# Attention's instructions and early transfers in the order of a table, 68 of them on another engine, three filler matmuls fewer

## The chip, the cores and the metric

The kernel runs on one core of a Trainium2 chip. The core has engines that each work through a queue of their own, in order: TensorE (PE, with the loading of weights shown as PEld), VectorE (DVE), ScalarE (ACT), GpSimd (POOL), and SyncE (SP), which issues nearly all transfers. The metric is the time of one execution on the device in microseconds (us), as the median of several runs.

## The reference

Attention over a window of 16 to either side and over one summary for each block of 32 positions (the maximum of the keys, the mean of the values), and behind it two expert layers with the same shape and different activations.

```python
def _attn_ref(q, k, v):                       # q, k, v: 2 x 8 x 768 x 64
...
    k_sum = k.reshape(B, H, nb, block, D).max(axis=3)
    v_sum = v.reshape(B, H, nb, block, D).mean(axis=3)
    scores_l = scale * np.matmul(q, k.transpose(0, 1, 3, 2))
...
    mask_l = np.abs(pos[:, None] - pos[None, :]) < window
    scores_s = scale * np.einsum('bhsd,bhnd->bhsn', q, k_sum)
    scores_s = scores_s + np.log(block)
...
    a = np.exp(scores_all)
    a = a / (np.sum(a, axis=-1, keepdims=True) + 1e-09)
...
    return np.matmul(a, v_all).astype(np.float32)

def _moe_ref(x, w_in, w_out):                 # x: 1536 x 512, d_ff 2048
    h = x @ w_in
    r = np.maximum(h, 0.0)
    g = r * r
    return (g @ w_out).astype(np.float32)

def _moe2_ref(x, w_in, w_out):
    h = x @ w_in
    g = h * (1.0 / (1.0 + np.exp(-1.702 * h)))
    return (g @ w_out).astype(np.float32)
```

## The kernel before

The kernel doesn't issue an instruction when its code is written. Each piece of work is an operation in a plan (`Plan.op`): an engine, a duration that the plan assumes, a function that issues the instructions, and the buffers it reads and writes. The plan gives every operation a start time by its own rules, and `emit` sorts all of them by that start and calls their functions. So the start times decide one thing alone: the order of the instructions in each engine's queue. What an instruction waits for follows from its buffers. Where several engines could do a piece of work, `soonest` takes the choice that the plan expects to end first. Operations are numbered (`seq`) in the order in which they are planned. Numbers 0 to 1199 are attention, the steps of the first expert layer that stand between its pieces, and the beginning of what follows.

The string `ORDER` lists the pieces of the front. Those that the text speaks of:

- `K`, `B`, `q`, `k`, `V`, `v`: transfers of parts of k, q and v. `T`, `tq`, `tk`: transposes on PE (L646 for k's first six blocks, L604 for q and k) and the copies from PSUM to `kw` and `qT`. `tq,1` is the second block of q, in two halves.
- `g,i,h`: for block i of 128 queries and half h of the heads the scores on PE (L735), the maximum passes on DVE (L750, each one operation a head, with its read-out), the exponentials of four heads on ACT (L765), the reciprocal (L779) and the multiply (L772) of the softmax. `h,i,h` is the same with all scores at once.
- `t,i`: transposes of the weights (L802), copies to `pT`, the weighted sum on PE (L814), and its split into a rounded part `xh` and a rest `xl` (L827).
- `w,f,z`: block f of an expert's weights: a transfer to `raw`, ACT scales it (L923), DVE joins parts (L927, L932), and ACT or DVE split it into a rounded `w` and a rest (L958 or L959, L963).
- `s,f,h` and `S,f`: one step of the first expert layer over half h of 512 tokens, or over all: 12 matmuls to `h` (L998), relu and square (L1012 to L1019), the rounded activations `gh` (L1026, L1027) and their low half `gl` (L1029), and one step later 12 matmuls to `acc` (L1053).

From 168 us on, the rest of both expert layers runs.

PE also gets filler matmuls, which multiply the identity by itself into a bank that nobody reads yet, so that PE is at work where the plan has gaps: `fill` puts them into gaps of the plan, and `WARM` adds groups at two given times. One filler is two matmuls in the trace (tile `warm`, L1774). The fillers need the identity, which POOL makes.

The lines behind the copies of the front, as an example of a choice of engines:

```python
    def copy(out, src, ps, key, cost=0.48):
        plan.soonest([("ACT", cost, False, lambda: nc.scalar.copy(out=out(), in_=src())),
                      ("DVE", cost * 1.26, False, lambda: nc.vector.tensor_copy(out=out(), in_=src()))],
                     reads=[(ps, 0)], writes=[*key, (ps, 0)])
```

Of the kernel before, what the change touches and what calls it, by code (L numbers as in the profile page):

```python
# [38 lines left out]
}  # L39
LAST = (2,), (0, 1), (3,)  # L40
SHAKE = (14, 0.15)
WARM = (15.52, 6), (21.24, 5)
KEPT = 10
LOW3 = 7.4999 / 2.0 ** 32
LESS = 99.0
# [91 lines left out]


class Op:
    __slots__ = ("eng", "start", "end", "fn", "seq", "far")  # L140


class Plan:
# [93 lines left out]
    def soonest(self, choices, reads=(), writes=(), after=()):  # L237


        best = None  # L240
        deps = self._deps(reads, writes, after)
        for eng, dur, port, fn in choices:
            if eng == "POOL" and port and self.alone:
                continue
            lines = (eng, "PORT") if port else (eng,)
            dur *= self.slack[1] if eng == "POOL" else 1.0
            end = self._place(lines, self._ready(eng, deps), dur) + dur
            if eng == "DVE":
                end += self.lean[0] if choices[0][0] == "ACT" else self.lean[1]
            if best is None or end < best[0]:  # L250
                best = end, eng, dur, port, fn
        _, eng, dur, port, fn = best
        return self.op(eng, dur, fn, reads=reads, writes=writes, after=after, port=port)

    @staticmethod
    def _deps(reads, writes, after):
# [43 lines left out]
                self.ops.append(o)  # L300

    def emit(self):
        for o in sorted(self.ops, key=lambda o: (o.start, o.seq)):
            o.fn()

# [2 lines left out]
def kernel(  # L308
# [1466 lines left out]

    plan.fill(0.27, keep_warm, first_ops["acc3"], WARM)
    with tc.manual_schedule():
# [30 lines left out]
```

## Time and profile before

| | us |
|---|---|
| median of 3 runs | 567.78 (567.07 to 567.97) |
| the profiled execution | 568.08 |
| its span, first to last instruction | 566.4 |
| PE busy in the span | 560.2 |
| DVE busy | 495.6 |
| ACT busy | 412.7 |
| POOL busy | 41.8 |

The span is the time between the first and the last instruction of the profiled execution; 1.7 us of that execution lie around it. Busy times are those of the whole span; the front of the kernel, up to some 35 us, looks different from the rest, and is read by stretches further down. A busy PE includes its fillers, and the ends of matmuls are modelled.

### The profile page before, as it was taken

The numbers are of one execution on the slowest core, as the hardware profiler recorded it, in microseconds if no ns is written. First come the engines' busy times: TensorE is split into PE (matmuls) and PEld (weight loads), VectorE is DVE, ScalarE is ACT, GpSimd is POOL, SyncE is SP. The second block draws the span as 40 slices with busy tenths as digits, with TensorE's granted clock in tenths as the row PEclk, the third lists the DMA queues.
The fourth block names the chain that finished last, engine by engine and source line by source line (L and its number), as shares of the span: only waits on it lengthen the run. The fifth ranks groups of instructions, "written<-read, shape, count | busy, mean of one in ns | idle before, by whom it ended". The sixth has DMA issues, their size and how long they took to land.

```text
span 566.4 us, 11027 instructions
## 1 busy us (share of the span) xinstructions
PE 560.2 (99%) x3838; PEld 481.3 (85%) x3838; DVE 495.6 (88%) x1110; ACT 412.7 (73%) x899; POOL 41.8 (7%) x112
## 2 busy tenths in 40 slices
PE   8999999999999999999999999999999999999997
PEld 8889988888878887888888888888888888899997
DVE  4788898888889899989999899998999999789974
ACT  4899889898896668777789757477366676677650
POOL 6143311211100000000000000000000000000000
PEclk9999999999999999999999999999999999999999
DMA  9999999886677864545558657576255555686723
GB/s 273 247 270 281 273 267 302 262 216 198 208 238 259 269 221 148 182 152 168 186 181 282 206 168 235 185 241 199 92 203 187 176 200 191 213 286 205 222 90 112
DMA packets 104663, 120.26 MB, mean 212 GB/s; under 512 B 28736, under 2 KB 72512, under 8 KB 104608
## 3 DMA queue, kind: packets, MB, share of 16 engines
q1 hardware_dynamic: 104416, 119.17, 67.1%
q0 software_dynamic: 192, 0.39, 0.4%
q8 instruction: 30, 0.49, 0.4%
q14 instruction: 25, 0.20, 0.1%
HBM read 86.64 MB, written 32.51 MB: 210 GB/s over the span
## 4 chain that ended last, share of the span: by engine, by line
PE 94%; SPq 1%; DMA 1%; DVE 1%; ACT 1%; issue 0%; DVEq 0%; ACTq 0%
PE acc L1440 14%; PE m L1440 12%; PE h L998 10%; PE acc L1053 8%; PE acc L1347 8%; PE acc L1345 7%; PE m L1345 5%; PE acc L998 5%; PE m L1347 4%; PE m L1055 4%; PE acc L1055 3%; PE h L1347 2%; PE h L1345 2%; PE m L802 2%; PE m L814 2%; PE m L998 1%
## 5 line engine op out<-in xcount | busy, mean ns | idle before, releaser
L963 DVE TENSOR_TENSOR w<-xw,w 128x512 fp32r<-128x512 f32 (+1 forms) x141 | 83.9, 609 | 2.7 <-ACT w L958 2.0
L958 ACT CAST w<-xw 128x512 fp32r<-128x512 f32 (+1 forms) x127 | 68.5, 552 | 23.0 <-DVE xw L932 15.9
L998 PE MATMUL h<-xh,w 128*128 128x512 f32 (+1 forms) x184 | 55.6, 364 | 0.0
L1440 PE MATMUL m<-top,w 128*128 128x512 f32 x210 | 53.5, 391 | 0.1
L932 DVE SCALAR_TENSOR_TENSOR xw<-raw,xw 128x512 uint32<-128x512 uint32 x67 | 45.8, 689 | 4.6 <-ACT raw L923 2.7
L923 ACT ACTIVATE raw<-raw 128x512 f32<-128x512 f32 x72 | 47.7, 679 | 1.0 <-DMA raw<-in_moe_w_in_dram 0.8
L1440 PEld LDWEIGHTS m<-top,w 128*128 128x128 f32 x210 | 38.7, 188 | 8.2 <-ACT r L363 0.5
L1440 PE MATMUL acc<-top,w 128*128 128x512 f32 x174 | 43.9, 390 | 0.0
L1053 PE MATMUL acc<-gh,w 128*128 128x512 f32 (+1 forms) x160 | 42.6, 353 | 0.0
L1440 PE MATMUL acc<-xh,w 128*128 128x512 f32 x124 | 42.1, 389 | 0.0
L1440 PEld LDWEIGHTS acc<-top,w 128*128 128x128 f32 x174 | 32.4, 188 | 6.5
L998 PEld LDWEIGHTS h<-xh,w 128*128 128x128 f32 x184 | 33.1, 189 | 5.6 <-issue 1.0
L765 ACT ACTIVATE sm<-sm,st 128x120 f32<-128x120 f32 x96 | 36.6, 385 | 0.2
L927 DVE TENSOR_SCALAR xw<-raw 128x512 uint32<-128x512 uint32 x67 | 29.1, 438 | 6.8 <-DMA raw<-in_moe_w_in_dram 5.4
L998 PE MATMUL h<-xl,w 128*128 128x512 f32 (+1 forms) x92 | 32.5, 353 | 0.0
L958 ACT CAST top<-gs 128x512 fp32r<-128x512 f32 x38 | 23.5, 618 | 11.3 <-DVE gs L947 3.0
L1053 PEld LDWEIGHTS acc<-gh,w 128*128 128x128 f32 x160 | 27.7, 189 | 4.4 <-issue 0.3
L963 DVE TENSOR_TENSOR top<-gs,top 128x512 fp32r<-128x512 f32 x41 | 27.9, 685 | 2.8 <-ACT top L958 2.6
L1347 PE MATMUL acc<-w,gh 128*128 128x256 f32 x136 | 28.0, 283 | 0.0
L1053 PE MATMUL acc<-gl,w 128*128 128x512 f32 (+1 forms) x80 | 27.8, 348 | 0.0
L1440 PEld LDWEIGHTS acc<-xh,w 128*128 128x128 f32 x124 | 23.3, 188 | 4.8
L998 PE MATMUL acc<-xh,w 128*128 128x512 f32 x80 | 26.1, 389 | 0.0
(300 smaller groups left out, 1501.6 us busy)
## 6 DMA issues: line engine op xcount, KB each, us to landing
raw<-in_moe_w_in_dram SPq DMA_DIRECT2D x36, 512.0 KB, 4.7
raw<-in_moe_w_out_dram SPq DMA_DIRECT2D x36, 512.0 KB, 4.6
w<-xw SPq DMA_DIRECT2D x50, 256.0 KB, 2.3
xw<-w SPq DMA_DIRECT2D x27, 256.0 KB, 2.8
w<-w SPq DMA_DIRECT2D x24, 256.0 KB, 2.8
r<-g SPq DMA_DIRECT2D x17, 256.0 KB, 3.7
vw<-in_v_dram SPq DMA_DIRECT2D x20, 192.0 KB, 4.7
g<-w SPq DMA_DIRECT2D x14, 256.0 KB, 2.0
```

Of the source, the lines that this page charges most:

```text
L765: nc.scalar.activation(out=s.t[:, h, :], in_=s.t[:, h, :], func=AF.Exp, bias=st.t[:, 0, h:h + 1], scale=-1.0, accum_out=st.t[:, 1, h:h + 1])
L923: nc.scalar.activation(out=top, in_=top, func=AF.Prelu, scale=-(2.0 ** -80), alpha=-(2.0 ** -32))
L927: plan.soonest([("DVE", 0.36, True, lambda: nc.vector.tensor_scalar(out=x.t, in0=raw.t[:, :, 0], scalar1=29, scalar2=None, op0=ALU.logical ...
L932: op("DVE", 0.64, lambda: nc.vector.scalar_tensor_tensor(out=x.t, in0=raw.t[:, :, 1], scalar=3, in1=x.t, op0=ALU.logical_shift_left, op1=A ...
L958: plan.soonest([("ACT", 0.09 + 0.44 * fr, False, lambda: nc.scalar.copy(out=hi.t[:, hc], in_=src())), ("DVE", 0.05 + 0.4 * fr, True, lambd ...
L963: eng.tensor_tensor(out=lo.t[:, lc], in0=src(), in1=hi.t[:, hc].bitcast(F32), op=ALU.subtract)
L998: nc.tensor.matmul(hp.t[:, cols], lhsT=w.t[:, kc * P:(kc + 1) * P], rhs=x.t[:, kc, cols], start=(kc == 0 and n == 0), stop=(kc == KC - 1 a ...
L1053: nc.tensor.matmul(a.t[:, cols], lhsT=w.t[:, j * P:(j + 1) * P], rhs=g.t[:, cols], **st)
L1055: nc.tensor.matmul(a.t, lhsT=g.t[:, j * P:(j + 1) * P], rhs=w.t, **st)
L1345: nc.tensor.matmul(b.t, lhsT=w.t[:, x + j * P:x + j * P + P], rhs=g.t, **st)
L1347: nc.tensor.matmul(b.t[:, (j % 2) * CH:(j % 2) * CH + CH], lhsT=g.t[:, j * P:j * P + P], rhs=w.t[:, x:x + CH], **st)
L1440: nc.tensor.matmul(bank.t, lhsT=a, rhs=rhs(b, kh), start=(begin and k == 0 and n == 0), stop=(k == 1 and n == 2), skip_group_check=True)
```

## The change

Two tables are added. `SHIFT` gives 1160 of the operations 0 to 1199 an offset that is added to the planned start before the sort, so it moves them in the queues of all engines, transfers included. `PICK` names 68 operations that were given to `soonest`, and takes the choice with that number instead: 35 go from ACT to DVE, 8 from DVE to ACT, 15 from DVE to POOL, 9 from POOL to DVE, one from POOL to ACT. The second group of `WARM` has two fillers instead of five. Buffers and banks of PSUM are still given out in planning, before the offsets, so who shares a buffer with whom stays as it was.

```diff
-WARM = (15.52, 6), (21.24, 5)
+WARM = (15.52, 6), (21.24, 2)
+SHIFT = {0: 1.001, 1: 1.499, 2: 4.8, 3: -0.749, 4: -4.578, 5: -1.226, 6: -0.7, 7: 0.111, 9: 0.101, 10: 6.4, 11: -0.9,
...
+PICK = {8: 1, 15: 1, 17: 1, 86: 1, 95: 0, 100: 0, 102: 0, 146: 0, 171: 1, 176: 1, 198: 1, 199: 1, 220: 0, 265: 1, 285:
...
 class Op:
-    __slots__ = ("eng", "start", "end", "fn", "seq", "far")
+    __slots__ = ("eng", "start", "end", "fn", "seq", "far", "alts")
...
-        return self.op(eng, dur, fn, reads=reads, writes=writes, after=after, port=port)
+        o = self.op(eng, dur, fn, reads=reads, writes=writes, after=after, port=port)
+        o.alts = choices
+        return o
...
     def emit(self):
+        for o in self.ops:
+            o.start += SHIFT.get(o.seq, 0.0)
+            if o.seq in PICK:
+                o.eng, _, _, o.fn = o.alts[PICK[o.seq]]
         for o in sorted(self.ops, key=lambda o: (o.start, o.seq)):
             o.fn()
```

Three places in the queues follow, as they stand in a row before and after. The line numbers of after are higher by 129 to 133, since the tables take lines.

The first is PE's queue around the transposes of q's second block (`m` from `qin`, L604 before, L733 after), with the scores of block 1 ahead of them. Before:

```order
L735 MATMUL acc_292<-kw,qT_283 64x120
L735 MATMUL m_294<-kw,qT_283 64x120
L1774 MATMUL warm<-ident 128x128 x6
L604 MATMUL m_318<-ident,qin_255 64x128 x8
L604 MATMUL m_329<-ident,qin_255 64x128 x8
L735 MATMUL acc_347<-kw,qT_283 64x120
L735 MATMUL h_349<-kw,qT_283 64x120
```

And after:

```order
L864 MATMUL acc_309<-kw,qT_284 64x120
L864 MATMUL m_311<-kw,qT_284 64x120
L733 MATMUL m_319<-ident,qin_211 64x128 x8
L1903 MATMUL warm<-ident 128x128 x6
L733 MATMUL m_336<-ident,qin_211 64x128 x8
L864 MATMUL acc_355<-kw,qT_284 64x120
L864 MATMUL acc_357<-kw,qT_284 64x120
```

The six fillers of the first group of `WARM` stood ahead of both halves and stand between them now. The scores of `g,0,1` (to `acc_347` and `h_349` before) have gone ahead of the transposes.

The second is DVE's queue at the same time, where the maximum passes of `g,1,0` (`sm_343`, in after `sm_351`) and of `g,0,1` (`sm_390`, in after `sm_376`) begin. Before:

```order
L963 TENSOR_TENSOR w_373<-xw_308,w_357 128x512
L750 ISA sm_343,st_344<-m_294,mask_74 128x120
L750 ISA st_344 128x1
L750 ISA sm_343,st_344<-m_294,mask_74 128x120
L750 ISA st_344 128x1
L750 ISA sm_390,st_391<-acc_347,mask_75 128x120
L750 ISA st_391 128x1
L750 ISA sm_390,st_391<-acc_347,mask_75 128x120
```

And after:

```order
L879 ISA sm_351,st_352<-m_311,mask_74 128x120
L879 ISA st_352 128x1
L493 COPY qT_372<-m_336 128x256
L879 ISA sm_376,st_377<-h_297,mask_75 128x120
L879 ISA st_377 128x1
L879 ISA sm_376,st_377<-h_297,mask_75 128x120
L879 ISA st_377 128x1
L879 ISA sm_351,st_352<-acc_355,mask_74 128x120
...
L879 ISA sm_376,st_377<-acc_295,mask_75 128x120
```

The copy of the second half of q's second block (`m_336`) was ACT's and stands on DVE now, ahead of the two passes of `g,0,1` and of the first of `g,1,1` (`acc_355`), which has gone between those two. The two subtractions of weights (L963) follow later.

The third is DVE's queue where the half-width steps `s,2,0` and `s,2,1` get their activations. In the row of before, the squares (`r`) and casts (`gh`) of these steps are ACT's (L1017, L1027), the subtractions (`gl`) POOL's (L1029), and DVE has weights and the softmax of block 5. After:

```order
L1061 SCALAR_TENSOR_TENSOR xw_1073<-raw_888,xw_1073 128x512
L1148 TENSOR_TENSOR r_1075<-r_1075 128x256
L1155 CAST gh_1090<-r_1075 128x256
L1158 TENSOR_TENSOR gl_1095<-r_1075,gh_1090 128x256
L1092 TENSOR_TENSOR w_1099<-xw_1073,w_1097 128x512
L1056 TENSOR_SCALAR xw_1114<-raw_972 128x512
L1148 TENSOR_TENSOR r_1119<-r_1119 128x256
L1061 SCALAR_TENSOR_TENSOR xw_1114<-raw_972,xw_1114 128x512
L1155 CAST gh_1140<-r_1119 128x256
L1158 TENSOR_TENSOR gl_1152<-r_1119,gh_1140 128x256
```

Six of the eleven half-width instructions that DVE gets in these steps are seen here, among the preparation of weights that was there before.

## Rows read from the trace of the kernel before

**Rows 1.** The page: the chain that ended last, shares of the span by engine.

```profile
PE 94%; SPq 1%; DMA 1%; DVE 1%; ACT 1%; issue 0%; DVEq 0%; ACTq 0%
```

**Rows 2.** Stretches: length, then PE, PEld, DVE, ACT, POOL busy; PEclk, DMA.

```profile
17.20:34.50 17.30, 17.18 (x330) 15.02 (x330) 14.27 (x83) 16.10 (x67) 4.89 (x12) 1.00 1.01 232
34.50:76.70 42.20, 42.19 (x461) 38.86 (x456) 35.65 (x93) 37.21 (x102) 15.23 (x28) 1.00 1.00 279
```

**Rows 3.** Timeline of PE, 0 to 24 us: start, length, line, tiles, count.

```profile
1.43 2.93 PE L1774 MATMUL warm<-ident 128*128 128x128 f32 x12 [1.43 <-POOL band L391]
4.29 1.12 PE L646 MATMUL acc<-ident,kin 128*64 128x128 f32 x8
...
8.12 1.97 PE L646 MATMUL acc<-ident,kin 128*64 128x128 f32 x32 [0.27 <-DMA kin<-in_k_dram]
...
14.96 1.60 PE L1774 MATMUL warm<-ident 128*128 128x128 f32 x12
17.21 1.97 PE L604 MATMUL m<-ident,qin 128*64 128x128 f32 x32 [0.65 <-DMA qin<-in_q_dram]
...
22.18 1.38 PE L1774 MATMUL warm<-ident 128*128 128x128 f32 x10
```

**Rows 4.** Timeline of ACT, 17 to 29 us.

```profile
21.27 0.39 ACT L765 ACTIVATE sm<-sm,st 128x120 f32<-128x120 f32 x1
...
28.30 0.59 ACT L363 COPY pT<-h 120x512 f32<-120x512 f32 x1
```

**Rows 5.** Timeline of DVE, 5 to 21 us.

```profile
5.36 0.48 DVE L927 TENSOR_SCALAR xw<-raw 128x512 uint32<-128x512 uint32 x1 [5.36 <-DMA raw<-in_moe_w_in_dram]
...
19.91 0.28 DVE L750 CUSTOM_DVE_ANT_0 sm<-acc,mask 128x120 f32<-128x120 f32 x1 [0.82 <-PE h L735]
...
20.12 0.28 DVE L750 CUSTOM_DVE_ANT_0 sm<-acc,mask 128x120 f32<-128x120 f32 x1
```

**Rows 6.** Groups by form, 0 to 170 us: count, busy us, mean ns.

```profile
L963 DVE TENSOR_TENSOR w<-xw,w 128x512 fp32r<-128x512 f32 x34 | 23.9, 711 | 2.5 <-ACT w L958 2.0
L772 DVE TENSOR_TENSOR sm<-sm,st 128x480 f32<-128x480 f32 x18 | 12.4, 691 | 1.8
L959 DVE CAST w<-xw 128x512 fp32r<-128x512 f32 x10 | 4.3, 426 | 1.4 <-PE h L998 1.1
L364 DVE COPY kw<-m 64x512 f32<-64x512 f32 x1 | 0.7, 683 | 0.0
L1014 DVE TENSOR_SCALAR r<-h 128x256 f32<-128x256 f32 x1 | 0.4, 418 | 0.0
...
L1029 POOL TENSOR_TENSOR gl<-r,gh 128x256 fp32r<-128x256 f32 x8 | 6.4, 799 | 14.1 <-ACT gh L1027 6.2 <-issue 3.9 <-PE acc L1053 3.0
```

**Rows 7.** Timelines of DVE and PE around 77 us.

```profile
75.97 0.68 DVE L1029 TENSOR_TENSOR gl<-r,gh 128x512 fp32r<-128x512 f32 x1
...
77.60 0.39 PE L1053 MATMUL acc<-gl,w 128*128 128x512 f32 x1
```

**Rows 8.** DVE's waits for ACT and POOL, 34.5 to 76.7 us: total us, times, longest.

```profile
DVE xw L932 <- ACT raw L923: 1.0, 2, 0.5
DVE w L963 <- ACT w L958: 0.8, 2, 0.5
DVE ks L683 <- ACT kw L363: 0.4, 1, 0.4
DVE st L779 <- POOL st L769: 0.4, 2, 0.2
```

**Rows 9.** The chain, 80 to 100 us: start, length, what, count.

```profile
90.13 2.94 PE h L998 x12
93.08 2.72 PE acc L1053 x12
```

**Rows 10.** Timelines of DVE and POOL around 38 us.

```profile
38.02 1.33 DVE L963 TENSOR_TENSOR w<-xw,w 128x512 fp32r<-128x512 f32 x1 [0.29 <-ACT w L958]
...
37.81 0.99 POOL L772 TENSOR_TENSOR sm<-sm,st 128x480 f32<-128x480 f32 x1 [0.30 <-DVE st L779]
```

121 rows, old and new, of tables (PICK, SHIFT) are left out of this document.

## The prediction

> **What bounds the kernel now.** I read the page's chain first [rows 1]: 94% of what ended last is TensorE (PE). Then the table by stage [rows 2]: from 34.5 us on the sum of PE's work is the whole stretch (42.19 of 42.20 us before 76.7 us), and the granted clock reads 1.00, the level of 2.4 GHz. So PE's work from there to the end is a fixed quantity, and every microsecond by which the front part ends earlier or later, or by which PE is made to wait later, goes straight into the time. The profiled run took 568.08 us for a span of 566.4; the median of the runs shown is 567.78, 0.3 us less. I make the sum on 568.08 and take off 0.3. A difference of about 0.2%, 1.1 us, is what a measurement of this kernel can tell from none.
>
> The front part is where PE has room. The timeline of PE [rows 3] shows filler matmuls ("warm"), 12, 12 and 10 of them in the three rows here, which do no useful work, and waits for transfers: 0.65 us at 17.21 for the second block of q. But in 17.2 to 34.5 us ScalarE (ACT) is busy 16.10 of 17.30 us and VectorE (DVE) 14.27 [rows 2]. What keeps PE waiting there is the softmax on those two. On ACT [rows 4] exponentials run in sets of four heads behind the copies of the transposed q: the second set, that of `g,0,1`, begins at 21.27, and the copy to `pT` for the first weighted sum at 28.30. The 1.20 us in which ACT is idle lie mostly ahead of the first set, so what delays the second set delays what follows.
>
> **The change, part by part.**
>
> Term 1, the front. PE waited for q's second block until 17.21 [rows 3]. Its two halves of 16 matmuls take 1.97 us together. Before, the 12 fillers stood ahead of both and were over while PE waited anyway. After, they stand between the halves, at 0.11 us apiece (12 of them in 1.60 us, 10 in 1.38, so 0.11 for one more, [rows 3]), 1.3 us. First half 17.21 to 18.2, fillers to 19.5, second half to 20.5. Nothing in the transfers ahead of q's block has become smaller, so I don't move 17.21. The copy of that second half has gone to DVE, ahead of three of the four maximum passes over scores that are ready. DVE is in order: it stands still until 20.5, copies for 0.42 (a 128x256 row of [rows 6]), and makes three passes of two operations, which start 0.21 us apart (19.91 and 20.12, [rows 5]), so 0.41 us each. The second set of exponentials can begin at 20.5 + 0.42 + 1.23 = 22.15 instead of 21.27: 0.9 us late. ACT's short gaps up to 28.30 close by that, of which I take a quarter of its 1.20 us; so the front ends 0.6 us later. That is the term: **+0.6**. Its lower bound is that the fillers don't hold up the second half: then its copy is over at 19.2 + 0.42 = 19.6, the passes at 20.85, and the set begins 0.4 us earlier than now: -0.4. The three fillers that go are six matmuls or 0.67 us, but they stand where PE waits for the last of v, so I give them nothing (-0.67 at most).
>
> Two things happen ahead of that. GpSimd (POOL) makes other constants before the identity that fillers need (0.5 to 0.7 us by the gaps ahead of the first filler, at 1.43, [rows 3]). And the first weight block is asked for ahead of k's short part, so PE's first transposes, at 4.29 now, start when that block has landed too: DVE takes it at 5.36 [rows 5]. The copies of k's first transposes go to DVE as well. Lateness of up to a microsecond there is covered by DVE's wait for 20.5; what it costs if more is the fourth rival.
>
> Term 2, DVE as the second bound. Count what stands ahead of the low half of step 4's activations (`gl` of S,4, line 1029) in DVE's queue: the same instructions as before, plus 21 that come from ACT and POOL, minus 7 that go. In: four copies of 128x256, one of 512 columns, two casts, one multiply, eleven half-width pieces of the first steps, and two adds of four columns, which I leave out: 4 x 0.42 + 0.68 + 2 x 0.43 + 0.69 + 11 x 0.42 = 8.5 us. Out: two subtractions, two multiplies, two copies and a cast: 2 x 0.71 + 2 x 0.69 + 0.42 + 0.68 + 0.43 = 4.3 us [rows 6]; copies and half-width pieces of 128x256 go by the one row of that shape. So 4.2 us more. Today that instruction ends at 76.65 (75.97 plus 0.68) and PE uses it at 77.60 [rows 7], 0.95 us later. With the front 0.6 us late, PE would want it at 78.2 and DVE have it at 76.65 + 0.6 + 4.2 = 81.45, less whatever of DVE's idle time the change fills. DVE idles 6.55 us of 34.5 to 76.7 [rows 2]. Which waits go? Those for ACT and POOL, whose queues lose what DVE gains: 1.0 + 0.8 + 0.4 + 0.4 = 2.6 us [rows 8]. Its other waits, for PE and for transfers, stay as far as I can see. 81.45 - 2.6 - 78.2 = 0.65: **+0.65**. The ends are 0 (from 3.25 us absorbed on) and +3.25 (none). Behind PE at that point stand matmuls alone, so it isn't won back.
>
> What speaks for the moves is real: ACT loses the same work, and POOL's half-width subtractions of 0.80 become shorter on DVE [rows 6]. That is worth something only where PE waits on ACT or POOL, and from 34.5 us on PE's sum leaves no such wait to see [rows 2].
>
> One price moves with the engine. At 38.02 a subtraction on DVE takes 1.33 us instead of 0.69, beside a POOL multiply that runs from 37.81 to 38.80 [rows 10]: with two inputs in SBUF it stood still until POOL was done. The Trainium skill, "SBUF — State Buffer", section "Who interferes with whom", states just this, a lock that whichever starts first keeps for its whole instruction; by that rule each of the two multiplies that go to POOL in the front could cost DVE up to 0.7 us, 1.4 us in all, and the trace agrees with its one pair. I take 0: in the order after, DVE has copies, maximum passes and reciprocals beside those two, with one input in SBUF at most, and the half-width subtractions that leave POOL (0.80 each, [rows 6]) free it later. The 1.4 stays in the range.
>
> Term 3, the order of PE's own work. Small tiles (scores, weighted sums, 64 columns) and full tiles of 128x128 alternate. In the chain [rows 9] twelve matmuls behind a score block take 2.94 us, the twelve behind them 2.72: leaving small tiles costs 0.22. By the order of PE's rows behind S,7 there are 10 such exits before and 13 after, since blocks that stood side by side are pulled apart: 3 x 0.22 = **+0.65**. No wait hides that on a full PE; bounds 0 and 0.7.
>
> The other moves reorder transfers and weight preparation with their consumers behind them by many microseconds; a dense PE hides them, and if a weight block came late, a step's twelve matmuls (2.72 us) would be next. I put nothing, with 1 us either way in the range.
>
> Sum: 0.6 + 0.65 + 0.65 = +1.9; 568.08 + 1.9 = 570.0 profiled, **569.7** as a median.
>
> **The rivals.**
>
> Faster. For it: ACT's load in the front, and g,0,1's scores stand ahead of q's second block and no longer behind it, so DVE's wait of 0.82 us for them at 19.91 can go [rows 5]. It decides where the second half's copy is over by 19.6: then the front gives 0.4 and the six filler matmuls 0.67, and the 0.9 us that the earlier scores spare DVE's passes comes off as well; if DVE also absorbs its 4.2 us and the exits cost nothing, 568.08 - 2.0 = 566.1, median 565.8. Against it: the fillers' place in PE's queue, and a DVE that must fill half and more of its idle time.
>
> No change that can be measured: the front is 0.3 early or late, DVE absorbs all, and the exits cost up to 0.65: 567.5 to 568.7.
>
> DVE takes over: nothing of the 4.2 us is absorbed, 0.6 + 3.25 + 0.65 = +4.5, median 572.3. The idle time that is there speaks against it.
>
> The clock. The first 12 fillers take 2.93 us and 12 later ones 1.60; 8 transposes from 4.29 take 1.12 and 32 from 8.12 only 1.97 [rows 3]. So matmuls run at half rate, as at 1.2 GHz, until about 7 us, though the clock reads 1.00 in the stretches of [rows 2]. After the change PE stands idle from about 3 us, behind two fillers, until k's short part lands near 5.3. If the rise comes later by that much, the next 32 transposes cost up to 2 us more; DVE's waits cover about 1, so +1 on the sum: 570.7. The Trainium skill, "TensorE: Matmul & The Clock Gate", Part 1, states that the throttled state is the default and that sustained activity releases it; by that rule the idle stretch delays the release, and I would add 1 us. The trace agrees that the first matmuls are slow; no stretch of it has an idle PE ahead of the rise.
>
> **Chances and range.** Slower, by terms 1 to 3: 0.33; DVE takes over, 0.07; the clock, 0.10, together 0.50. No change: 0.23. Faster: 0.27. The ends: 565.5 leaves out what is beyond the faster case, some 0.1; 572.6 lies just above the full price of DVE and leaves out 0.1 in which two causes add up. The likeliest case by itself: 568.9 to 571.0.
>
> **What would show it.** Right: in the new trace the fillers run between the two halves of q's transposes, with DVE idle before the copy to `qT`, the second set of exponentials at about 22.1 us and the copy to `pT` at 28.9; PE waiting for `gl` between 40 and 80 us; DVE busy for more than 38 us of 34.5 to 76.7, against 35.65 now. Wrong: exponentials earlier than 21, or PE's waits ahead of 76.7 us no larger than now, which would mean that DVE absorbed what it was given.

## The result, and the profile after

| | before | after |
|---|---|---|
| median, us | 567.66 (5 runs) | 572.23 (5 runs) |
| lowest to highest | 566.86 to 567.97 | 571.73 to 572.84 |
| profiled execution, us | 568.08 | 572.01 |
| its span | 566.4 | 570.3 |

The ratio is 1.0077, with a 95% interval from 1.0064 to 1.0090: the change costs 3.6 to 5.1 us, 4.4 in the middle. The forecast was 569.7, slower, with a range up to 572.6. So the direction was right and the time lies just inside the range, but the loss is more than twice the one worked out. That it lies inside is luck: the upper end was set by the price of DVE taking over (572.3), and that didn't happen.

The stretches of after come first (length, then PE, PEld, DVE, ACT, POOL busy), to be held against [rows 2]:

```profile
17.20:34.50 17.30, 15.95 (x292) 13.50 (x290) 14.62 (x72) 15.47 (x59) 5.41 (x12) 1.00 1.01 241
34.50:76.70 42.20, 42.20 (x526) 39.36 (x516) 38.36 (x120) 36.83 (x105) 13.84 (x27) 1.00 0.91 255
```

From 34.5 us on PE is as full as before: 42.20 of 42.20 us. DVE has taken its extra work (38.36 us, 35.65 before) and PE shows nothing of it. The room that PE lost is ahead of 34.5 us. Its timeline there, against [rows 3]:

```profile
2.16 1.22 PE L1903 MATMUL warm<-ident 128*128 128x128 f32 x4 [2.16 <-POOL ident masks.py:199]
5.79 1.12 PE L775 MATMUL acc<-ident,kin 128*64 128x128 f32 x8 [2.41 <-DMA kin<-in_k_dram]
6.84 2.08 PE L1903 MATMUL warm<-ident 128*128 128x128 f32 x8
8.85 1.12 PE L775 MATMUL h<-ident,kin 128*64 128x128 f32 x8
9.90 0.80 PE L1903 MATMUL warm<-ident 128*128 128x128 f32 x2
10.63 1.09 PE L775 MATMUL acc<-ident,kin 128*64 128x128 f32 x16
...
16.06 1.04 PE L733 MATMUL h<-ident,qin 128*64 128x128 f32 x16
...
19.72 1.09 PE L733 MATMUL m<-ident,qin 128*64 128x128 f32 x16
20.74 1.60 PE L1903 MATMUL warm<-ident 128*128 128x128 f32 x12
22.28 1.09 PE L733 MATMUL m<-ident,qin 128*64 128x128 f32 x16
```

Read the duration beside the count. Eight fillers at 6.84 take 2.08 us, twelve at 20.74 take 1.60; 8 transposes at 5.79 take 1.12, 16 at 10.63 take 1.09. So PE works at half rate, as at 1.2 GHz, until it reaches the row of 10.63, and at the rate of 2.4 GHz from there. Before, the rise came among the fillers that start at 6.20. The trace's own records of the granted clock say the same: the first of them, of 1.00, begins 10.57 us into the span here and 7.27 us before. Ahead of that first record there is none, and a stretch without a record reads 1.00 in the column PEclk. Ahead of the rise stand, in the changed kernel, four filler matmuls and then 2.41 us in which PE waits for k's short part. The fillers are not in `SHIFT`: k's first transposes were moved ahead of the planned start of four of the first six, which now stand behind the wait they could have filled.

VectorE and ScalarE behind it (the rows that answer to [rows 4, 5]), two fences:

```profile
23.42 0.42 DVE L493 COPY qT<-m 128x256 f32<-128x256 f32 x1 [1.88 <-PE m L733]
```

```profile
24.89 0.40 ACT L894 ACTIVATE sm<-sm,st 128x120 f32<-128x120 f32 x1 [0.64 <-DVE st L879]
...
31.66 0.59 ACT L492 COPY pT<-h 120x512 f32<-120x512 f32 x1
```

DVE stands still for 1.88 us ahead of the copy to `qT`, as foretold, but at 23.42 and not at 20.5. The second set of exponentials begins at 24.89 (21.27 before), the copy to `pT` at 31.66 (28.30). Lateness of this size is there by the time q's first block is transposed (16.06, 12.54 before), and from there to the second set it takes 8.83 us, 8.73 before. That these two are alike hides a gain and a loss, which e9_no_warm1 will take apart.

PE's waits up to 180 us, in total, with count and longest:

```profile
PE acc L775 <- DMA kin<-in_k_dram: 2.4, 1, 2.4
PE warm L1903 <- POOL ident masks.py:199: 2.2, 1, 2.2
PE acc L864 <- ACT qT L492: 0.7, 1, 0.7
PE acc L943 <- ACT pT L492: 0.7, 1, 0.7
PE acc L1184 <- ACT gh L1156: 0.2, 1, 0.2
```

No wait for `gl`, and none for DVE. The low half of step 4 on DVE and its first use on PE, the answer to [rows 7]:

```profile
78.30 0.69 DVE L1158 TENSOR_TENSOR gl<-r,gh 128x512 fp32r<-128x512 f32 x1
...
80.63 0.40 PE L1182 MATMUL acc<-gl,w 128*128 128x512 f32 x1
```

It ends at 78.99, 1.64 us ahead of its use; before it was 0.95. And the chain from 120 to 125 us, where a weighted sum (L943) and a score block (L864) that stood side by side have three matmuls between them:

```profile
121.60 1.08 PE m L943 x32
122.68 0.89 PE acc L1182 x3
123.57 0.98 PE m L864 x32
124.55 0.89 PE acc L1182 x3
```

Three full matmuls that follow small tiles take 0.89 us each time; by the 2.72 us for twelve of [rows 9] they would take 0.68. From 34.5 to 165 us there are 18 exits with such a loss of 0.2 us (14 before).

Four marks on the timelines show where each kernel stands: PE's first transpose of q's first block, the second set of exponentials on ACT, PE's first matmul of step `s,1,0`, and the end of the span. The last column is the span less that matmul. Each row is one profiled execution, and executions of the same kernel differ by 1 us and more, so some tenths in it tell nothing by themselves.

| kernel | q | second set | `s,1,0` | span | rest |
|---|---|---|---|---|---|
| before | 12.54 | 21.27 | 34.67 | 566.35 | 531.68 |
| after | 16.06 | 24.89 | 37.91 | 570.27 | 532.36 |
| e1_front | 16.10 | 24.93 | 38.24 | 569.60 | 531.36 |
| e2_back | 12.38 | 20.41 | 33.63 | 567.02 | 533.39 |
| e3_fillers_first | 12.90 | 21.72 | 34.64 | 566.96 | 532.32 |
| e7_k_first | 13.81 | 22.65 | 35.57 | 568.29 | 532.72 |
| e9_no_warm1 | 16.55 | 24.07 | 36.99 | 569.95 | 532.96 |
| e12_best | 13.09 | 20.61 | 33.53 | 566.04 | 532.51 |

Of the 3.92 us between the spans of before and after, 3.24 are lost ahead of `s,1,0` and 0.68 behind it.

### The profile page after: what moved, and what is told of

It is laid out like the page before. It is cut to its first block, busy times and chain, and to the rows that moved or that the text cites. A ratio compares the mean times of both kernels' runs of the same rounds, so it can differ in the third digit from the quotient of the medians.

```text
span 570.3 us, 10983 instructions
## 1 busy us (share of the span) xinstructions
PE 560.5 (98%) x3832; PEld 479.7 (84%) x3832; DVE 504.8 (89%) x1131; ACT 400.3 (70%) x873; POOL 54.4 (10%) x117
## 4 chain that ended last, share of the span: by engine, by line
PE 92%; DVE 3%; ACT 2%; DMA 2%; issue 0%; SPq 0%; DVEq 0%
PE acc L1569 14%; PE m L1569 12%; PE h L1127 8%; PE acc L1476 8%; PE acc L1474 7%; PE acc L1182 6%; PE m L1474 5%; PE acc L1127 5%; PE m L1476 4%; PE m L1184 4%; PE acc L1184 3%; PE h L1476 2%; PE h L1474 2%; PE m L864 1%; PE m L931 1%; DMA raw<-in_moe_w_out_dram 1%
## 5 line engine op out<-in xcount | busy, mean ns | idle before, releaser
L1092 DVE TENSOR_TENSOR w<-xw,w 128x512 fp32r<-128x512 f32 (+1 forms) x135 | 80.2, 608 | 1.2 <-ACT w L1087 0.5
L1087 ACT CAST w<-xw 128x512 fp32r<-128x512 f32 (+1 forms) x116 | 61.8, 546 | 20.5 <-DVE xw L1061 12.8
L1127 PE MATMUL h<-xh,w 128*128 128x512 f32 (+1 forms) x184 | 57.6, 364 | 0.0
L1061 DVE SCALAR_TENSOR_TENSOR xw<-raw,xw 128x512 uint32<-128x512 uint32 x67 | 47.0, 703 | 5.2 <-ACT raw L1052 2.6
L1182 PE MATMUL acc<-gh,w 128*128 128x512 f32 (+1 forms) x160 | 43.9, 360 | 0.0
L894 ACT ACTIVATE sm<-sm,st 128x120 f32<-128x120 f32 x96 | 36.7, 385 | 3.5 <-DVE st L879 3.4
```

The lines of the kernel that those rows point to most:

```text
L894: nc.scalar.activation(out=s.t[:, h, :], in_=s.t[:, h, :], func=AF.Exp, bias=st.t[:, 0, h:h + 1], scale=-1.0, accum_out=st.t[:, 1, h:h + 1])
L1061: op("DVE", 0.64, lambda: nc.vector.scalar_tensor_tensor(out=x.t, in0=raw.t[:, :, 1], scalar=3, in1=x.t, op0=ALU.logical_shift_left, op1=A ...
L1087: plan.soonest([("ACT", 0.09 + 0.44 * fr, False, lambda: nc.scalar.copy(out=hi.t[:, hc], in_=src())), ("DVE", 0.05 + 0.4 * fr, True, lambd ...
L1092: eng.tensor_tensor(out=lo.t[:, lc], in0=src(), in1=hi.t[:, hc].bitcast(F32), op=ALU.subtract)
L1127: nc.tensor.matmul(hp.t[:, cols], lhsT=w.t[:, kc * P:(kc + 1) * P], rhs=x.t[:, kc, cols], start=(kc == 0 and n == 0), stop=(kc == KC - 1 a ...
L1182: nc.tensor.matmul(a.t[:, cols], lhsT=w.t[:, j * P:(j + 1) * P], rhs=g.t[:, cols], **st)
```

## The experiments

The kernels ran in three groups, each beside runs of the kernel before. Its median was 567.70, 568.20 and 568.26 in them, so ratios are compared; the last column is the ratio less 1, times 567.7.

| kernel | ratio (95% interval) | us against before |
|---|---|---|
| after | 1.0077 (1.0064 to 1.0090) | +4.4 |
| e1_front | 1.0067 (1.0053 to 1.0081) | +3.8 |
| e2_back | 1.0029 (1.0018 to 1.0039) | +1.6 |
| e3_fillers_first | 1.0041 (1.0026 to 1.0057) | +2.3 |
| e4_tq_whole | 1.0089 (1.0074 to 1.0104) | +5.1 |
| e5_four_blocks | 1.0085 (1.0063 to 1.0107) | +4.8 |
| e6_no_pick | 1.0336 (1.0320 to 1.0353) | +19.1 |
| e7_k_first | 1.0039 (1.0027 to 1.0052) | +2.2 |
| e8_before_warm2 | 1.0006 (0.9992 to 1.0020) | +0.3 |
| e9_no_warm1 | 1.0046 (1.0032 to 1.0060) | +2.6 |
| e10_back_four | 1.0010 (1.0001 to 1.0019) | +0.6 |
| e11_pick_back | 1.0032 (1.0020 to 1.0043) | +1.8 |
| e12_best | 0.9994 (0.9983 to 1.0004) | -0.3 |

### Which part of the order costs: e1_front, e2_back

```diff
+SHIFT = {n: s for n, s in SHIFT.items() if n < 250}
+PICK = {n: c for n, c in PICK.items() if n < 250}
```

> The changed order and engines for operations 0 to 249 alone (up to some 45 us), the rest as before. Theory: nearly all that the change costs is lost ahead of 60 us, first of all because TensorE's clock rises at 10.4 us and no longer at 7.2; then +2.7 of the +4.0 us that the two profiles show as lost between their first and last stage stays: about 570.4. Rival, the loss is that of VectorE's and TensorE's later order: 568.5 or less.

e2_back has `n >= 250` in both lines and five fillers in the second group of `WARM`.

> The changed order and engines for operations 250 to 1199 alone, the front with its fillers as before. Theory: only more exits from small to full tiles and a wait for activations remain, +1.3 us: 569.0. Rival one, VectorE's extra work is what costs: 570 and more, with waits of TensorE for gl. Rival two, the later moves cost nothing: 567.7.

The front alone costs 3.8 us, the later part alone 1.6; the two intervals (3.0 to 4.6 and 1.0 to 2.2) overlap in their sum with the whole. So most of the loss is the front's, as theory said, and more than the 2.7 that I gave it. In e2_back PE waits for no `gl`, so rival one is out; behind 34 us it waits 0.7 us for ScalarE's copies. Its profile begins `s,1,0` 1.04 us earlier than that of before and takes 1.71 us more from there. These 1.71 need not all be its own order's: in e12_best, where everything from operation 250 on is as before and `s,1,0` also comes 1.14 us earlier, the rest takes 0.83 us more too. An earlier front was only partly passed on in these two profiles.

### The clock: e3_fillers_first, e7_k_first

e3_fillers_first puts the first six fillers ahead of k's first transposes:

```diff
+SHIFT.update({3125: -0.1, 3126: -0.45, 3127: -0.8, 3128: -1.15})
```

> The changed kernel with its first six fillers ahead of k's first transposes, so that TensorE works from 2.2 to 4.7 us and is idle for 1 us instead of 2.4. Theory, the idle stretch is what puts off the clock: it rises near 8 us, q's first block is transposed some 2.5 us earlier, and about 2 us come back: 570.2. Rival, the clock rises as late as in the changed kernel, at about 10.4, since TensorE still stands idle before k lands at 5.75: only the eight filler matmuls that no longer stand between k's transposes come back, 0.9 to 1.7 us there and less than 1 at the end, 571.5.

e7_k_first leaves the fillers and takes back two moves, those of the identity (operation 0) and of k's short part (1):

```diff
+SHIFT.update({0: 0.0, 1: 0.0})
```

> The changed kernel with the identity first on GpSimd and k's short part asked for ahead of the first weight block, as in the kernel before; the fillers stay where they are. TensorE then waits for k until about 3.7 us and no longer until 5.75. Theory, what follows the idle stretch is worked through at half rate until the clock rises, so the rise comes with the end of the wait: near 8.4 instead of 10.4, and about 2 us come back: 570.2. Rival, the rise doesn't move with the wait: less than 0.7 back, 571.5 or more.

PE's timeline of e3_fillers_first:

```profile
2.16 2.93 PE L1904 MATMUL warm<-ident 128*128 128x128 f32 x12 [2.16 <-POOL ident masks.py:199]
5.59 1.09 PE L776 MATMUL acc<-ident,kin 128*64 128x128 f32 x8 [0.50 <-DMA kin<-in_k_dram]
6.49 0.62 PE L776 MATMUL h<-ident,kin 128*64 128x128 f32 x8
7.04 0.49 PE L1904 MATMUL warm<-ident 128*128 128x128 f32 x2
...
12.90 1.04 PE L734 MATMUL h<-ident,qin 128*64 128x128 f32 x16
```

The second 8 transposes take 0.62 us and no longer 1.12: the clock has risen by 6.5 us, where its first record begins too (6.52). k's transposes begin 1.3 us later than before (5.59, 4.29), q's only 0.36 (12.90, 12.54). The nine executions of this kernel run from 568.7 to 572.3 us and the profiled one is the fastest, so the profile shows more of the gain than the median; why the others took longer isn't shown. PE's timeline of e7_k_first:

```profile
3.73 1.12 PE L776 MATMUL acc<-ident,kin 128*64 128x128 f32 x8 [1.08 <-DMA kin<-in_k_dram]
4.78 2.08 PE L1904 MATMUL warm<-ident 128*128 128x128 f32 x8
6.79 1.12 PE L776 MATMUL h<-ident,kin 128*64 128x128 f32 x8
7.84 0.61 PE L1904 MATMUL warm<-ident 128*128 128x128 f32 x2
8.38 1.09 PE L776 MATMUL acc<-ident,kin 128*64 128x128 f32 x16
```

Here the wait ends 2.06 us earlier than in the changed kernel and the rise comes 2.25 us earlier (by the rows of 16 transposes, 8.38 and 10.63; by the records of the clock, 8.12 and 10.57). Both gave back what was expected, 2.1 and 2.2 us of 4.4, and both rivals, which kept the rise near 10.4, are out. The two don't give back the same thing. In e7_k_first the work from k's first transposes to q's takes 10.08 us, nearly the 10.27 of the changed kernel, and only begins earlier; in e3_fillers_first it begins when it did and takes 7.31.

### The fillers between the halves: e4_tq_whole, e9_no_warm1

```diff
-WARM = (15.52, 6), (21.24, 2)
+WARM = (15.2, 6), (21.24, 2)
```

> The changed kernel with the first group of WARM ahead of both halves of q's second block, as in the kernel before. Theory (term 1): the copy of the second half on VectorE and the second set of exponentials, at 24.89 in the changed kernel, come up to 1.4 us earlier, and 0.6 to 1.3 us come back: 571.2. Rival, both halves come later behind the fillers and ScalarE's first set too, so nothing comes back: 572.2.

The rival holds, with a ratio that is no better than that of the change. ACT's sets of exponentials in e4_tq_whole, the first and the second:

```profile
23.39 0.41 ACT L894 ACTIVATE sm<-sm,st 128x120 f32<-128x120 f32 x1
...
25.20 0.40 ACT L894 ACTIVATE sm<-sm,st 128x120 f32<-128x120 f32 x1
```

With the fillers ahead of both halves the first set is late too (23.39, 21.82 in the changed kernel), and the second follows behind it. Of these 1.57 us 0.46 were there by q's first transposes (16.52, 16.06), since the clock rose later in this execution; the rest is the fillers'. So it isn't the place that costs, but that nothing waits there any more. e9_no_warm1 leaves the group out:

```diff
-WARM = (15.52, 6), (21.24, 2)
+WARM = (15.52, 0), (21.24, 2)
```

> The changed kernel without the first group of WARM, the six fillers (twelve matmuls, 1.5 us) that stand between the two halves of q's second block. Theory (term 1): the second half, VectorE's copy of it and the second set of exponentials, 24.89 in the changed kernel, come 1.5 us earlier, and 0.9 to 1.4 us come back: 571.1. Rival: what stood behind them waits for ScalarE's first set or VectorE anyway, 0.4 or less back: 571.8 to 572.3.

DVE's copy and ACT's second set in e9_no_warm1:

```profile
22.22 0.42 DVE L493 COPY qT<-m 128x256 f32<-128x256 f32 x1 [0.20 <-PE m L733]
```

```profile
24.07 0.41 ACT L894 ACTIVATE sm<-sm,st 128x120 f32<-128x120 f32 x1
```

DVE's idle time ahead of the copy falls from 1.88 to 0.20 us. From q's first transpose to the second set it is 7.52 us (24.07 less 16.55) where the change has 8.83, and to `s,1,0` 20.44 where it has 21.85. So the changed order saves some 1.2 us of the 8.73 of before, in which PE waits 0.65 us for q's second block, and the fillers take that back. By the ratio 1.8 us come back, with some 1.1 us to either side, which agrees with the theory's 0.9 to 1.4.

### The later exits: e5_four_blocks, e10_back_four

```diff
+for n, s in ((441, 1.1), (515, 4.0), (720, 0.3), (759, 0.4)):
+    SHIFT[n] += s
```

> The changed kernel with four blocks of TensorE's later order moved so that small tiles stand side by side again (the scores of h,7,0 next to transposes, the first matmuls of sv,1 next to their two fellows, the weighted sums of t,7 and t,6 next to the scores of h,11,0 and h,8,0). In the profile of the changed kernel 18 exits from tiles of 64 rows or columns to full tiles cost 0.2 us each, in that of before 14. Theory (term 3): four exits fewer, 4 x 0.21 = 0.85 us back: 571.4. Rival, a full tile stands in those places anyway for a wait that the order hides: 572.2.

The time didn't fall, though the interval (3.6 to 6.1 us against before) leaves room for the 0.85 us. PE's waits in e5_four_blocks that the changed kernel has not:

```profile
PE m L735 <- issue: 0.4, 1, 0.4
PE m L933 <- ACT pT L494: 0.3, 1, 0.3
```

Exits that cost 0.2 us fell from 18 to 14, and they were worth their price: from the first full matmul behind the scores of `h,5,0` to the first behind the second transposes of `t,6` it takes 59.91 us in the changed kernel (70.33 to 130.24) and 59.22 here (70.87 to 130.09), 0.69 less, with three of the four exits in it. Behind that PE, being earlier, waits 0.3 us for ScalarE's copy to `pT`, and ahead of it one stop of 0.4 us stands among transposes at 36.7 us, for which the trace names nothing. So the exits are paid as term 3 says, and taking them out is worth less than their sum. The same edit on e2_back:

> The changed order and engines for operations 250 to 1199 alone (569.3 when it ran), with the four blocks of TensorE's order moved so that small tiles stand side by side. Theory: the four exits, 0.85 us, come back where no other wait takes their place: 568.5, and the profile shows 14 exits that cost 0.2 us and no more than 0.3 us of new waits. Rival, as in the run with the whole change: a wait for ScalarE's copy to pT near 141 us or one like it takes all of it: 569.3.

The ratio is lower by 0.19% than that of e2_back, 1.1 us, with intervals that touch. But the profiles don't show it: with 13 such exits the span is 567.7, where that of e2_back is 567.0. The profiled execution of e10_back_four is one of its slower ones (569.45 us, the median is 569.09), that of e2_back one of its faster (568.74, 569.34). PE's longest waits behind 34 us in e10_back_four are

```profile
PE m L935 <- ACT kw L496: 0.6, 1, 0.6
PE m L935 <- ACT pT L496: 0.6, 1, 0.6
PE acc L947 <- ACT pT L496: 0.4, 1, 0.4
```

So what the four exits are worth in the whole time stays between nothing and 1.1 us.

### The engines: e6_no_pick, e11_pick_back

```diff
+PICK = {}
```

> The changed kernel with its order and its fillers, and every operation on the engine that it had before. Theory: VectorE's extra work is hidden behind TensorE (no wait of TensorE for it is seen behind 35 us), and the front is late for another reason: 571.5 to 572.6, as the changed kernel. Rival one, the moved work costs: below 571.2. Rival two, it pays for part of the loss, and without it ScalarE is the bound: 573 and more.

This is the miss of the study: rival two's direction, at many times its size. Three of PE's waits in e6_no_pick:

```profile
PE m L1185 <- DVE gl L1159: 2.4, 1, 2.4
PE h L1128 <- DVE r L1144: 2.4, 1, 2.4
PE m L932 <- DVE st L880: 1.6, 1, 1.6
```

DVE is late without the moves that give it work: from 135 to 200 us it stands 9.4 us in five waits for casts of `w` on ACT. With 35 instructions back on ACT, those casts stand behind other work in ACT's queue, and DVE, in order, behind them. In the longest of the five, 5.0 us, ACT itself waits ahead of the cast, 2.3 us for a transfer. A part of the 19.1 us is the clock again: the granted clock reads 0.83 from 160 to 170 us, where PE is busy for 7.67 of 10 us, 0.89 from 190 to 200 and 0.94 from 200 to 210, which by these figures is worth some 3 us (an estimate). How the rest comes about is argued from the waits and not tested. The offsets of `SHIFT` and the engines of `PICK` are one solution; the run says what the order costs without its engines, and not what the engines cost.

For that, the engines of the later part were tried on the order of before, with the fillers of before:

```diff
+SHIFT = {}
+PICK = {n: c for n, c in PICK.items() if n >= 250}
```

> The kernel before with the engines of the changed one for operations 250 to 1199 and no change of order or fillers. Theory (term 2 in its lower bound): VectorE's idle time takes up the work that moves to it, no wait of TensorE for it ahead of 170 us, and the time is that of before, 567.5 to 568.5. Rival one, VectorE is late with a low half (gl): 569.5 to 571. Rival two, an order and a choice of engines that were not made for each other block the queues as they did when the order came without the engines: 573 and more.

It is 1.8 us slower (1.1 to 2.4), which is rival one's time without its mechanism: PE waits for no `gl`. What it waits for from 34 to 180 us:

```profile
PE m L933 <- ACT pT L494: 0.3, 1, 0.3
PE h L1129 <- ACT r L1143: 0.2, 1, 0.2
```

Its profile reaches `s,1,0` 0.6 us earlier than that of before (at 34.07) and takes nearly 2 us more behind it. The waits that are seen, for ACT, make up 0.5 us of that; the rest of it has no shown cause. So the moves of engines don't pay on the old order, and in the new one DVE's part is hidden.

### The second group and a combination: e8_before_warm2, e12_best

```diff
+SHIFT, PICK = {}, {}
```

> The kernel before with the second group of WARM of two fillers and no other change. The prediction: six filler matmuls fewer where TensorE waits for the last part of v anyway, nothing: 567.7. Rival, TensorE and the chain behind it are free 0.3 to 0.67 us earlier: 567.0 to 567.4.

No difference that can be told. Its profile has a stop of PE in the middle of 32 transposes, the rows of PE at 32 us:

```profile
31.93 0.38 PE L734 MATMUL m<-ident,kin 128*64 128x128 f32 x2
34.23 1.96 PE L734 MATMUL m<-ident,kin 128*64 128x128 f32 x30 [1.92 <-issue]
```

The profile of before has no such stop. The last kernel takes what helped:

```diff
-WARM = (15.52, 6), (21.24, 2)
+WARM = (15.52, 0), (21.24, 2)
+SHIFT = {n: s for n, s in SHIFT.items() if n < 250}
+PICK = {n: c for n, c in PICK.items() if n < 250}
+SHIFT.update({0: 0.0, 1: 0.0, 3125: -0.1, 3126: -0.45, 3127: -0.8, 3128: -1.15})
```

> A combination: the changed order and engines for operations 0 to 249 alone, with the identity and k's short part first as before, six fillers ahead of k's first transposes, and no fillers between the halves of q's second block; from operation 250 on all as before. Theory: the clock rises as early as in the kernel before, the weights of the later order's 1.6 us are gone, and the changed front with its earlier transfers gains up to 0.9 us: 566.8 to 567.5, faster than both. Rival: the changed front gives nothing even so: 567.7 to 568.3.

Within the measurement of before, by 0.3 us (from -1.0 to +0.2). The changed front, cleared of its two losses, reaches `s,1,0` 1.14 us sooner, but behind it PE waits 0.6 us for a copy to `kw` on DVE at 40 us, and little reaches the end. Four of its twelve executions (568.5 to 569.3 us) have a mean granted clock of 0.997, the others (566.8 to 568.6) one of 1.00; none of the four was profiled. Held against e1_front, whose part from operation 250 on is the same, the three repairs take 3.8 us to nothing that can be told, so no large loss of the front is left without a name. None of these versions beats the kernel before by an amount that was measured.

## Why the prediction was right, and where it was too small

The direction came out, but the reasons behind it only in part: a rival held at 0.10 is the largest part of the loss, and of the three terms one was too small, one nothing and one about right.

**The clock.** This is the step that failed in size. I held it a rival with a chance of 0.10 and a price of 1 us. It is half of the loss or more: 2.1 us come back when fillers stand ahead of k's transposes, 2.2 when k comes first, each with an interval of some 1.1 us to either side. The mechanism was named rightly, down to the two fillers and the idle stretch; I took PE for idle until about 5.3 us, and it was so until 5.79. The price was wrong in two places. I charged the late rise to the next 32 transposes. But the fillers that were left behind the wait ran at half rate too, ten matmuls among the 26 from 5.79 to the rise, so that the 96 transposes of k, with 16 filler matmuls between them and not 8, take 10.27 us from the first (5.79 to 16.06) where before they took 8.25 (4.29 to 12.54), on top of a start that is 1.50 us late. e3_fillers_first undoes the first of these, e7_k_first the second. And I covered 1 us of it by DVE's wait for the second half at 20.5, which moved along with everything else. By the Trainium skill, "TensorE: Matmul & The Clock Gate", Part 1, the throttled state is the default and sustained activity releases it; the trace agrees: the rise came later where PE had stood idle longer, at 8.1 us behind a wait of 1.08 us that ended at 3.7, and at 10.6 behind one of 2.41 us that ended at 5.8.

**Term 1, +0.6.** The mechanism was right, as e9_no_warm1 shows: fillers between the halves, DVE idle ahead of the copy, the second set late by 1.31 us (8.83 less 7.52). The base was wrong. I kept q's second block at 17.21. In the changed kernel PE came to it at 19.72 without a wait, in e3_fillers_first at 16.55 without one, and in e2_back, with the front of before, at 16.34: 17.21 was the landing of one execution, and the fillers covered no wait at all. That they stand between the halves is not the point (e4_tq_whole); that they stand there at all is.

**Term 2, +0.65.** Its lower bound was the right one: nothing. DVE is busy for 2.7 us more from 34.5 to 76.7, its waits for ACT and POOL fell from 2.6 [rows 8] to 0.5 us, and `gl` comes 1.64 us ahead of its use. The queue in front of it grew by 4.2 us and it came only 2.3 us later (78.30, 75.97), while PE came 3 us later (80.63, 77.60). What I had named as a sign that DVE absorbs the work, no larger waits of PE, is what the profile shows.

**Term 3, +0.65.** Right in mechanism: there are four more exits at 0.2 us, and the stretch of e5_four_blocks gave back 0.69 us for three of them. That 0.68 us are lost behind `s,1,0`, near the 0.65, shows less than it seems: in the table above the rest goes from 532.32 to 533.39 us among kernels with the changed later part, and from 531.36 to 532.51 with that of before.

Of the sum, 0.6 + 0.65 + 0.65, the first was thus a fifth of the 3.24 us that the front lost, the second nothing, and the third near what its exits cost. On the timelines the front's loss adds up otherwise: 1.50 us for the late start of k's transposes, 2.02 for the half rate and the fillers among them, 1.31 for the fillers between q's halves, less 1.21 that the order saves besides (8.73 less 7.52). That makes 3.62 us at the second set and, a little of it won back, 3.24 at `s,1,0`. The other rivals fall: no faster kernel, no DVE that takes over, although 572.3 was that rival's time.

## What to carry to other kernels

Before you reorder queues by a table, list what is not in the table: here the fillers kept their planned times while the work around them moved, so that they stood behind a wait that they should have filled and, later, in a place where nothing was waited for. In the first microseconds, price a late first transfer by the rate at which TensorE works after it, as the rows of the trace show it, and not by the wait alone. An order and a choice of engines that were found together are worth nothing apart.

## What was not expected of the hardware

The same queue of PE ahead of the rise gave different rises. The eight fillers at 6.2 us take 1.66 us in the profile of before; in e2_back, with the same work ahead of them, PE's row is

```profile
5.88 1.16 PE L1905 MATMUL warm<-ident 128*128 128x128 f32 x8
```

They run at full rate there from the first on. By the first record of the granted clock the rise comes at 5.49 us in e2_back, 5.80 in e8_before_warm2, 5.81 in e11_pick_back, 6.14 in e10_back_four and 7.27 in before, all with the front of before, and the stretches of before and e2_back ahead of it read 1.00 in the column PEclk all the same. So near a kernel's start the length of equal matmuls tells the rate, and the column doesn't. And PE stopped for 0.4 to 1.9 us among transposes for which the trace shows no wait (e5_four_blocks, e8_before_warm2); the profile calls it issue, and what it waits for wasn't settled.
